# Uneven column parts in the tail of a two-stage attention and soft-MoE kernel: 288 + 224 instead of 256 + 256, and eight instead of twelve row blocks stored by parts

## The chip, the cores and the metric

The kernel runs on one core of a Trainium2 chip. Its engines work side by side and meet through semaphores: PE multiplies matrices, DVE and ACT do elementwise work and move results out of PSUM, POOL (GpSimd) masks and issues the loads that convert types, and SP issues the stores. Sixteen DMA engines move all the data between memory and the core's SBUF. The metric is the device time of one execution in microseconds (us).

## What is computed

Inputs are q, k and v of 4 batches x 8 heads x 768 positions x 64 columns. The first stage is an attention in which every query keeps 6 of 24 chunks of 32 keys, chosen by an upper bound on the score. Its output, as 3072 tokens x 512 columns, goes into a soft mixture of experts:

```
logits = x @ phi                      # 3072 x 32: 8 experts, 4 slots each
slot_input = softmax over tokens(logits).T @ x
for e in range(8):
    h = relu(slot_input[e] @ w1[e])   # w1[e]: 512 x 1024
    slot_out[e] = h @ w2[e]           # w2[e]: 1024 x 512
out = softmax over slots(logits) @ slot_out    # 3072 x 512, float32
```

So no output row can be formed before all slots are known, since each token mixes all 32 of them; and each column of `slot_out` needs the same column of all eight `w2`. The kernel uses the last point: the output can be finished for some columns while the weights of the other columns are still on their way. 6.29 MB of output are stored at the end.

## The kernel before

The work goes in 16 pairs of heads. For each pair, lists of step names (`PLAIN`, `REST`, ..., `FINAL`) set by hand in which order the instructions are put into the engines' queues. All this runs until about 121 us of the span; the change touches only what comes at the end.

Weights are loaded by POOL's queue, which also converts them from float32 to bfloat16. Fourteen of the sixteen matrices (`w1` of all experts, `w2` of the first six in the order `LATE`) come whole. The last two, `w2` of the experts 7 and 4, come in eight pieces, `load_w_half(0)` to `(7)` (L160): first the columns y = 1 (the right part) of both, then the columns y = 0 of both, each part in two pieces of 512 rows. Pieces 0 to 3 are issued from the lists of the last two pairs (`lh:0` to `lh:3`), pieces 4 to 7 after them. All pieces wait their turn in one queue.

The tail runs so, in the order of PE's queue:

- `experts_in` (L932): slot input times `w1`, in two halves of the hidden columns, with `relu` on ACT and `hidden_T` between.
- Part y = 1: `experts_out(1, f)` (L973) for the four experts with whole columns of the PE array, `shared_out(1, f)` (L999) for three experts that are spread over the column groups (the second-last of them from the pieces `w_half`), `last_expert_out(1)` (L1009) for the very last expert, all summed in `so_ps`. ACT scales the sum into the bfloat16 `so_sb[1]` (L1059).
- `out_half(m, 1, ...)` (L1046) for the first `BYHALF` entries of `ROWS`: PE mixes the slots for 128 tokens at a time, DVE and ACT in turn scale the result into the SBUF tile `o_rows` (L1029, L1026), SP stores it (L1050).
- Part y = 0 in the same way, from `experts_out(0, f)` on, summed in `so_last`, scaled on DVE (L1068); then `out_half(m, 0, ...)` for the same rows.
- The remaining rows in full width, 512 columns at once (PE L1078, store L1081). After the first of these, `last_rows` prepares the factors of the last batch: six transposes (L548), their copy on DVE (L556), six sums (L823) and a reciprocal (L959).

`ROWS` lists (first block of 128 tokens, number of blocks). In a group of w blocks, token p*w + x of the group sits in partition p, so a store of full rows writes w x 2048 bytes in one run per partition, and a store of one column part writes runs of its own width. The entry decides the size of the packets that the DMA engines handle.

```
    ROWS = [(2 * m, 2) for m in range(4)] + [(8, 4), (12, 2), (14, 4), (18, 6)]
    BYHALF = 5
```

With this, 12 blocks of 128 rows are stored by column parts (each of them twice, 256 columns or 1024 bytes wide) and 12 blocks in full. SP has 14 stores: 5 of part y = 1, 6 of part y = 0, 3 of full rows.

Of the kernel before, what the change touches and what calls it, by code (L numbers as in the profile page):

```python
# [9 lines left out]
F32 = mybir.dt.float32  # L10
BF16 = mybir.dt.bfloat16
# [9 lines left out]
P = 128  # L21
# [38 lines left out]
def kernel(  # L60
# [15 lines left out]
    Dm, NS = moe_phi.shape  # L76
    E, F = moe_w1.shape[0], moe_w1.shape[2]
    SPE = NS // E
    LATE = [0, 1, 2, 3, 5, 6, 7, 4]
    NDG, NFG = Dm // P, F // P  # L80
    EARLY = 14
    LAST = NPAIR - 1
    WIN, HOME = 6 * SPE, 4 * SPE

    ctx.enter_context(tc.manual_schedule())
    static = ctx.enter_context(tc.tile_pool(name="static", bufs=1))
# [2 lines left out]
    p_sc = ctx.enter_context(tc.tile_pool(name="p_sc", bufs=2, space=PSUM))  # L89
    p_at = ctx.enter_context(tc.tile_pool(name="p_at", bufs=1, space=PSUM))  # L90
# [15 lines left out]
    w_sb = []  # L106
# [45 lines left out]
    w_half = {}  # L152
# [3 lines left out]
    def load_w_half(n):  # L156

        e, y, a = HALVES[n]
        src = moe_w2[e].rearrange("(a p x) d -> a p x d", p=P, x=4)
        nc.gpsimd.dma_start(  # L160
            out=w_half[e, y][:, 4 * a:4 * a + 4, :], in_=src[a, :, :, y * Dm // 2:(y + 1) * Dm // 2])

    def load(i, nm, n=1):

# [18 lines left out]
    for t, src in zip(stage, (k, q)):  # L183
# [4 lines left out]
        out=ident, in_=ident, compare_op=ALU.not_equal, fill=1.0, base=0,  # L188
# [623 lines left out]
            return False  # L812
        return True

    ROWS = [(2 * m, 2) for m in range(4)] + [(8, 4), (12, 2), (14, 4), (18, 6)]

    def tokens(t0, w, x):
        return cT_all[:, t0:t0 + w].rearrange("p n c -> p (n c)").rearrange("p (k x) -> p x k", x=w)[:, x]

    def col_sums(ps, b):  # L820
        cols = [(t0, w, x) for t0, w in ROWS if t0 // NQT == b for x in range(w)]
        for n, c in enumerate(cols):
            nc.tensor.matmul(ps[:, n:n + 1], lhsT=tokens(*c), rhs=live, start=True, stop=True)  # L823
# [4 lines left out]
    for i in range(1, NPAIR):  # L828
        if i == NPB + 1:
            nc.vector.tensor_reduce(live, once, axis=AX.X, op=ALU.max)  # L830
        if i >= EARLY:
            wt = ctx.enter_context(tc.tile_pool(name=f"wt{i}", bufs=1))
            for y in range(2):
                w_half[LATE[i - E], y] = wt.tile([P, NFG, Dm // 2], BF16, name=f"w_half{i}_{y}")
        order = FINAL if i == LAST else BEFORE_LAST if i == LAST - 1 else PLAIN if i <= NPB else (
            REST, LOGITS, SLOTS, AFTER)[i % NPB]
        for what in order.split():
            if what.startswith("lh:"):
                load_w_half(int(what[3:]))
# [23 lines left out]
    for n in range(4, len(HALVES)):  # L863
        load_w_half(n)
# [19 lines left out]
    for n, part in enumerate((high(mneg), mneg_lo)):  # L884
        nc.tensor.matmul(
            lg2, lhsT=part.broadcast_to([NS, P]), rhs=rep.broadcast_to([NS, NQT, NS]),
            start=False, stop=(n == 1), skip_group_check=True,
# [34 lines left out]

    h_sb = tail.tile([P, 2, 512], BF16, name="h_sb")
    so_all = tail.tile([P, Dm], BF16, name="so_all")
    so_sb = [so_all[:, y * Dm // 2:(y + 1) * Dm // 2] for y in range(2)]
    h_ps.append(p_sc.tile([P, 2, 512], F32, name="h_ps1", tag="sc"))

    def experts_in(f, g):
# [26 lines left out]
    def last_rows():  # L955
        moe_ct(BL)
        ps = p_tp.tile([P, NQT], F32, name="cs_ps", tag="tp")
        col_sums(ps, BL)
        nc.vector.reciprocal(inv_b, ps)  # L959

    HD = Dm // 2
    so_ps = p_at.tile([P, 2, 512], F32, name="so_ps", tag="at")[:, 0, :HD]
    so_last = p_sc.tile([P, HD], F32, name="so_last", tag="sc")

    hT = hT_pad.rearrange("p f e c -> p f (e c)")

# [2 lines left out]
    def experts_out(y, f):  # L969
        for fg in range(f * 4, (f + 1) * 4):  # L970
            for e in range(4):
                w0 = fg * Dm + y * HD
                nc.tensor.matmul(  # L973
                    outs[y][e * CH:(e + 1) * CH, :], lhsT=hT_pad[:, fg, e, :],
                    rhs=w_sb[E + e][:, w0:w0 + HD], start=(fg == 0), stop=False,
                )

    SHARED = [
# [6 lines left out]
    def window(e, j):  # L985
        return e * CH + HOME - (e - j) * SPE

    def shared_out(y, f):
        for n in range(3):
            for j in range(4):  # L990
                e, fg = SHARED[j][n]
                fg += f * 4
                c0 = window(e, j)
                if e == LATE[-2]:
                    rhs = w_half[e, y][:, fg, :]
                else:
                    w0 = fg * Dm + y * HD
                    rhs = w_sb[E + LATE.index(e)][:, w0:w0 + HD]
                nc.tensor.matmul(  # L999
                    outs[y][j * CH:(j + 1) * CH, :], lhsT=hT[:, fg, c0:c0 + CH],  # L1000
                    rhs=rhs,
                    start=False, stop=False,
                )

    def last_expert_out(y):
        for fg in range(NFG):
            j = fg % 4
            c0 = window(LATE[-1], j)
            nc.tensor.matmul(  # L1009
                outs[y][j * CH:(j + 1) * CH, :], lhsT=hT[:, fg, c0:c0 + CH],  # L1010
                rhs=w_half[LATE[-1], y][:, fg, :],
                start=False, stop=(fg >= NFG - 4),
            )
# [9 lines left out]
    homes = {"sc": p_sc, "tp": p_tp, "at": p_at}  # L1023
# [6 lines left out]

    w_ctx.close()
    op = ctx.enter_context(tc.tile_pool(name="op", bufs=1))
    BYHALF = 5
    o_tiles = [op.tile([P, w, Dm], F32, name=f"o_rows{t0}") for t0, w in ROWS]

    def rows(m):
        t0, w = ROWS[m]
        return out[t0 * P:(t0 + w) * P, :].rearrange("(p x) d -> p x d", x=w)

    def out_half(m, y, tags):  # L1040
        cols = slice(y * HD, (y + 1) * HD)
        t0, w = ROWS[m]
        for x in range(w):
            tag = tags[m % 2 ^ x // 2][x % 2]
            ps = homes[tag].tile([P, HD], F32, name="oh_ps", tag=tag)
            nc.tensor.matmul(ps, lhsT=tokens(t0, w, x), rhs=so_sb[y], start=True, stop=True)  # L1046
            (scaled_dve, scaled_act)[x % 2](o_tiles[m][:, x, cols], ps, t0 + x)
            if x == w - 1 or x % 2 and y == 0:
                xs = slice(x - 1 if y == 0 else 0, x + 1)
                nc.sync.dma_start(out=rows(m)[:, xs, cols], in_=o_tiles[m][:, xs, cols])  # L1050

    experts_out(1, 0)
    shared_out(1, 0)
    hidden_T(1)
    slot_sums()
    experts_out(1, 1)
    shared_out(1, 1)
    last_expert_out(1)
    nc.scalar.activation(so_sb[1], outs[1], func=ACT.Copy, scale=zinv)  # L1059
    TAGS = (("tp", "tp"), ("sc", "at"))  # L1060
    for m in range(BYHALF):
        out_half(m, 1, TAGS)
    for f in range(2):
        experts_out(0, f)
    for f in range(2):
        shared_out(0, f)
    last_expert_out(0)
    nc.vector.tensor_scalar_mul(so_sb[0], outs[0], zinv)  # L1068
    for m in range(BYHALF):
        out_half(m, 0, TAGS)  # L1070

    n = 0
    for m in range(BYHALF, len(ROWS)):
        t0, w = ROWS[m]
        for x in range(w):
            tag = ("sc", "tp", "tp", "sc", "at")[n % 5]
# [4 lines left out]
        nc.sync.dma_start(out=rows(m), in_=o_tiles[m])  # L1081
        if m == BYHALF:
            last_rows()
# [30 lines left out]
```

## Time and profile before

| what | us |
|---|---|
| median of 3 runs (156.21 to 156.38) | 156.22 |
| the profiled execution | 155.95 |
| its span, first to last instruction | 154.2 |
| PE busy (89% of the span) | 136.8 |
| ACT busy (79%) | 121.5 |
| DVE busy (78%) | 120.4 |
| POOL busy (63%) | 97.5 |

Times in the views count from the start of the span. The profile names each DMA queue: q0 is POOL's (loads), q1 is SP's (stores, and two loads at the very start). A view of a stretch gives the number of packets, their bytes and rate, and each queue's share of the time of all 16 DMA engines; a share over 100% means that packets overlap on an engine. Sizes count the bytes written, so a converting load reads twice what is shown. "Time to landing" counts from the issue of a DMA until its last data is confirmed. The chain of waits is followed back from the last instruction: at each step to what released it.

### The profile page before, as it was taken

What the parts mean: (1) busy time and instruction counts of PE and PEld (TensorE: products, weight loads), DVE (VectorE), ACT (ScalarE), POOL (GpSimd) and SP (SyncE); (2) the same over time, 40 slices, a digit from 0 to 9 for tenths busy, and PEclk for the clock granted to TensorE, in tenths of its full rate; (3) what the DMA queues carried; (4) which work ended last, traced back from release to release, by engine and by line L of the source; (5) the groups of instructions that cost most, each with busy time, mean ns of one, the idle gap of its engine ahead of it and who ended that gap; (6) DMA issues with size and microseconds to landing.
All of it is one profiled execution on the core that took longest, in us unless ns stands there. A gap on an engine that the chain in (4) does not pass through costs nothing.

```text
span 154.2 us, 6098 instructions
## 1 busy us (share of the span) xinstructions
PE 136.8 (89%) x2513; PEld 91.6 (59%) x2513; DVE 120.4 (78%) x445; ACT 121.5 (79%) x167; POOL 97.5 (63%) x200
## 2 busy tenths in 40 slices
PE   7889999999999998999999799999989899776700
PEld 2444566767667686666667575767767655453300
DVE  4777988989899998999999999999767551449710
ACT  3678999999999999899999979999997133428700
POOL 6966698974976798885847938794694971000000
PEclk9999999999999999999999999999999999999975
DMA  4999999999999999999999999999999999999996
GB/s 140 207 188 206 206 189 194 215 179 196 209 217 193 199 205 189 198 205 212 205 190 198 209 202 199 206 184 213 217 191 218 211 197 198 181 266 353 371 429 255
DMA packets 45579, 33.31 MB, mean 216 GB/s; under 512 B 26224, under 2 KB 41584, under 8 KB 45296
## 3 DMA queue, kind: packets, MB, share of 16 engines
q0 software_dynamic: 41328, 25.86, 115.4%
q1 hardware_dynamic: 4224, 7.08, 12.5%
q8 instruction: 19, 0.31, 0.7%
q14 instruction: 8, 0.07, 0.1%
HBM read 52.49 MB, written 6.29 MB: 381 GB/s over the span
## 4 chain that ended last, share of the span: by engine, by line
PE 55%; POOL 13%; DMA 9%; DVE 8%; issue 5%; ACT 5%; DVEq 0%; SPq 0%; POOLq 0%; ACTq 0%
PE at_ps L382 12%; PE sc_ps L334 12%; PE sc_ps L344 9%; DMA w_half<-in_moe_w_dram 7%; PE tr_ps L225 6%; PE xT_ps L404 4%; POOL e_sb L368 4%; ACT e_sb L358 3%; PE ub_ps L284 3%; DMA w_sb<-in_q_dram 2%; PE ns_ps L316 2%; POOL v_t L174 2%; DVE o_rows L1029 2%; POOL w_half L160 1%; POOL w_sb L150 1%
## 5 line engine op out<-in xcount | busy, mean ns | idle before, releaser
L358 ACT ACTIVATE e_sb<-sc_ps 128x1024 bf16<-128x1024 f32 (+2 forms) x96 | 83.2, 932 | 4.7 <-PE sc_ps L344 4.5
L368 POOL TENSOR_SCALAR_AFFINE_SELECT e_sb<-e_sb 128x256 bf16<-128x256 bf16 x96 | 37.9, 415 | 15.6 <-ACT e_sb L358 15.2
L334 PE MATMUL sc_ps<-qT,kT 64*128 64x384 bf16 (+3 forms) x260 | 37.5, 306 | 0.7 <-ACT e_sb L358 0.6
L344 PE MATMUL sc_ps<-nsT,smask 64*128 64x384 bf16 (+2 forms) x296 | 37.6, 284 | 0.1
L382 PE MATMUL at_ps<-v_t,e_sb 128*128 128x65 bf16 x630 | 25.9, 193 | 1.0 <-DVE x_sb L395 0.8
L382 PEld LDWEIGHTS <-e_sb 128*128 128x128 bf16 x630 | 22.0, 97 | 5.1 <-issue 4.0
L305 DVE MAX8 mx<-ub_ps 128x8 f32<-128x8 f32 (+1 forms) x192 | 16.9, 165 | 5.6 <-PE ub_ps L294 5.1
L334 PEld LDWEIGHTS <-kT 64*128 64x128 bf16 x260 | 13.5, 93 | 8.4 <-issue 1.8
L174 POOL DMA_DIRECT2D v_t<-in_v_dram x16 | 16.9, 1056 | 1.1 <-PE sc_ps L344 0.9
L344 PEld LDWEIGHTS <-smask 64*128 64x128 bf16 x296 | 14.9, 95 | 3.1 <-issue 0.4
L395 DVE TENSOR_TENSOR x_sb<-at_ps,inv 128x768 bf16<-128x768 f32 (+3 forms) x18 | 15.6, 869 | 0.6
L244 DVE TENSOR_REDUCE mm<-kT 128x24 bf16<-128x768 bf16 x16 | 15.1, 944 | 0.1
L250 DVE TENSOR_REDUCE mm<-kT 128x24 bf16<-128x768 bf16 x16 | 15.1, 943 | 0.0
L235 ACT COPY qT<-tr_ps 128x768 bf16<-128x768 bf16 x16 | 13.0, 813 | 1.5 <-PE tr_ps L225 1.5
L235 ACT COPY kT<-tr_ps 128x768 bf16<-128x768 bf16 (+1 forms) x16 | 12.7, 793 | 0.6 <-PE tr_ps L225 0.6
L150 POOL DMA_DIRECT2D w_sb<-in_moe_w_dram x14 | 10.1, 724 | 0.0
L415 DVE COPY xT_sb<-xT_ps 128x768 bf16<-128x768 bf16 (+1 forms) x16 | 8.6, 535 | 2.0 <-PE xT_ps L404 2.0
L215 PE MATMUL warm_ps<-ones_sq 128*128 128x512 bf16 x27 | 8.7, 446 | 1.1 <-DVE ones_sq L180 1.1
L284 PEld LDWEIGHTS <-qpn 128*128 128x128 bf16 x192 | 6.1, 96 | 4.9 <-issue 3.8
L284 PE MATMUL ub_ps<-bd,qpn 128*128 128x48 bf16 x192 | 7.9, 184 | 0.8 <-issue 0.5
L404 PE MATMUL xT_ps<-ident,x_sb 128*128 128x128 bf16 x96 | 8.4, 220 | 0.0
L1026 ACT ACTIVATE o_rows<-oh_ps,inv_a 128x256 f32<-128x256 f32 x12 | 5.0, 470 | 3.5 <-PE oh_ps L1046 2.7
(171 smaller groups left out, 222.9 us busy)
## 6 DMA issues: line engine op xcount, KB each, us to landing
w_sb<-in_moe_w_dram POOLq DMA_DIRECT2D x14, 1024.0 KB, 18.3
v_t<-in_v_dram POOLq DMA_DIRECT2D x16, 192.0 KB, 15.1
out_dram<-o_rows SPq DMA_DIRECT2D x10, 256.0 KB, 3.0
w_half<-in_moe_w_dram POOLq DMA_DIRECT2D x8, 256.0 KB, 11.2
k_in<-in_k_dram POOLq DMA_DIRECT2D x5, 384.0 KB, 13.3
q_in<-in_q_dram POOLq DMA_DIRECT2D x5, 384.0 KB, 12.3
out_dram<-o_rows SPq DMA_DIRECT2D x1, 1536.0 KB, 6.0
out_dram<-o_rows SPq DMA_DIRECT2D x2, 512.0 KB, 3.9
```

The costliest lines, as they stand in the source:

```text
L174: nc.gpsimd.dma_start(out=v_t[i % NV][:, :, :, :D], in_=v[b, 2 * j:2 * j + 2].rearrange("h (g p) d -> p h g d", p=P),)
L235: copy(t.rearrange("d (p g) -> d p g", g=NQT)[:, :, g0:g1], ps.rearrange("d g p -> d p g"),)
L244: nc.vector.tensor_reduce(mm[:, 0, 0, :], kT, axis=AX.X, op=ALU.min)
L250: nc.vector.tensor_reduce(mm[:, 1, 0, :], kT, axis=AX.X, op=ALU.max)
L284: nc.tensor.matmul(o, lhsT=qpn[:, x, t * P:(t + 1) * P], rhs=bd[:, x], start=(t == 0 and x == 0), stop=False,)
L305: nc.vector.max(mx[:, a, :], ub[:, a, :max(8, 4 * t + 4)])
L334: nc.tensor.matmul(ps[:, h, c:c + w], lhsT=kT[r, kg * P:(kg + 1) * P], rhs=qT[r, qs], start=True, stop=False,)
L344: nc.tensor.matmul(ps[:, h, c + (f - t0) * P:c + (l - t0) * P], lhsT=smask[r, x, kg].rearrange("p a b -> p (a b)"), rhs=nsT[r, (f - x * NJ ...
L358: nc.scalar.activation(e[:, :, :w], st.pop(("scps", i, g))[:, :, :w], func=ACT.Exp, scale=scale)
L368: nc.gpsimd.affine_select(out=e[:, :, c:c + P], in_=e[:, :, c:c + P], compare_op=ALU.is_ge, fill=0.0, base=0, pattern=[[0, 2], [1, P]], ch ...
L382: nc.tensor.matmul(o, lhsT=st["e", i, g][:, h, c:c + P], rhs=v_t[i % NV][:, h, kg, :D + 1], start=(kg == 0), stop=(kg == t),)
L395: nc.vector.tensor_tensor(st["x", b][:, t0:t1, 2 * j:2 * j + 2, :].rearrange("p t h d -> p h t d"), at[:, :, :, :D], inv.broadcast_to([P, ...
```

## The change

The last two weights are cut at column 224 instead of 256: y = 0 gets columns 0 to 223, y = 1 columns 224 to 511. The first-loaded part y = 1 is thus 288 columns wide, the last-loaded part 224. All tiles, matmuls and stores of a part take its width. `ROWS` is cut anew: six groups of 2 blocks, then 4, 2 and 6; the first four groups (8 blocks) are stored by parts, the other 16 blocks in full. For y = 1, the first group's two blocks are stored one by one; for the others one store per group. And the 32 matmuls `experts_out(0, f)` are moved on PE's queue from behind the first part's output to a place ahead of `last_expert_out(1)`.

```
+    COLS = [slice(0, 224), slice(224, Dm)]
+    CW = [c.stop - c.start for c in COLS]
...
-            out=w_half[e, y][:, 4 * a:4 * a + 4, :], in_=src[a, :, :, y * Dm // 2:(y + 1) * Dm // 2])
+            out=w_half[e, y][:, 4 * a:4 * a + 4, :], in_=src[a, :, :, COLS[y]])
...
-    ROWS = [(2 * m, 2) for m in range(4)] + [(8, 4), (12, 2), (14, 4), (18, 6)]
+    ROWS = [(2 * m, 2) for m in range(6)] + [(12, 4), (16, 2), (18, 6)]
...
-                w_half[LATE[i - E], y] = wt.tile([P, NFG, Dm // 2], BF16, name=f"w_half{i}_{y}")
+                w_half[LATE[i - E], y] = wt.tile([P, NFG, CW[y]], BF16, name=f"w_half{i}_{y}")
...
-    so_sb = [so_all[:, y * Dm // 2:(y + 1) * Dm // 2] for y in range(2)]
+    so_sb = [so_all[:, c] for c in COLS]
...
-    HD = Dm // 2
-    so_ps = p_at.tile([P, 2, 512], F32, name="so_ps", tag="at")[:, 0, :HD]
-    so_last = p_sc.tile([P, HD], F32, name="so_last", tag="sc")
+    so_ps = p_at.tile([P, 2, 512], F32, name="so_ps", tag="at")[:, 0, :CW[1]]
+    so_last = p_sc.tile([P, CW[0]], F32, name="so_last", tag="sc")
...
-                w0 = fg * Dm + y * HD
+                w0 = fg * Dm + COLS[y].start
                 nc.tensor.matmul(
                     outs[y][e * CH:(e + 1) * CH, :], lhsT=hT_pad[:, fg, e, :],
-                    rhs=w_sb[E + e][:, w0:w0 + HD], start=(fg == 0), stop=False,
+                    rhs=w_sb[E + e][:, w0:w0 + CW[y]], start=(fg == 0), stop=False,
...
-    BYHALF = 5
+    BYHALF = 4
...
-        cols = slice(y * HD, (y + 1) * HD)
+        cols = COLS[y]
...
-            ps = homes[tag].tile([P, HD], F32, name="oh_ps", tag=tag)
+            ps = homes[tag].tile([P, CW[y]], F32, name="oh_ps", tag=tag)
...
-            if x == w - 1 or x % 2 and y == 0:
-                xs = slice(x - 1 if y == 0 else 0, x + 1)
+            if x == w - 1 or m == 0 and y == 1:
+                xs = slice(x if m == 0 and y == 1 else 0, x + 1)
                 nc.sync.dma_start(out=rows(m)[:, xs, cols], in_=o_tiles[m][:, xs, cols])
...
     experts_out(1, 1)
     shared_out(1, 1)
+    for f in range(2):
+        experts_out(0, f)
     last_expert_out(1)
     nc.scalar.activation(so_sb[1], outs[1], func=ACT.Copy, scale=zinv)
     TAGS = (("tp", "tp"), ("sc", "at"))
     for m in range(BYHALF):
         out_half(m, 1, TAGS)
-    for f in range(2):
-        experts_out(0, f)
     for f in range(2):
         shared_out(0, f)
     last_expert_out(0)
```

More of the change, by code (lines that the diff above doesn't have):

```diff
@@ L996, in shared_out @@
                 else:
-                    w0 = fg * Dm + y * HD
-                    rhs = w_sb[E + LATE.index(e)][:, w0:w0 + HD]
+                    w0 = fg * Dm + COLS[y].start
+                    rhs = w_sb[E + LATE.index(e)][:, w0:w0 + CW[y]]
                 nc.tensor.matmul(
```

## The prediction

> **What bounds the kernel now.** I read the page's slices first, for the engine that is full while the kernel ends; then the chain of waits over the tail, then the stores on SP's queue, then the DMA queues stretch by stretch.
>
> ```profile
> DMA  4999999999999999999999999999999999999996
> GB/s 140 207 188 206 206 189 194 215 179 196 209 217 193 199 205 189 198 205 212 205 190 198 209 202 199 206 184 213 217 191 218 211 197 198 181 266 353 371 429 255
> ```
>
> Busy tenths and rate of the DMA engines in 40 slices: they are full in every slice but the first and the last, and the rate doubles in the last ones, where stores replace loads. The chain of waits, from the last weight on:
>
> ```profile
> 127.14 10.44 DMA w_half<-in_moe_w_dram
> 137.63 0.32 PE so_last L1009 x4
> 137.97 0.49 DVE so_all L1068
> 138.51 0.41 PE oh_ps L1046 x2
> 138.94 0.84 ACT o_rows L1026 x2
> ...
> 144.54 2.06 DVE o_rows L1029 x3
> ```
>
> The last weight piece lands at 127.14 + 10.44 = 137.58; 1.86 us later (139.44) SP issues the first store of the second column part. SP's queue at the first store of the first part, the first of the second, and the last store of all:
>
> ```profile
> 134.09 0.62 SPq L1050 DMA_DIRECT2D out_dram<-o_rows  x1
> 139.44 0.53 SPq L1050 DMA_DIRECT2D out_dram<-o_rows  x1
> 147.33 0.33 SPq L1081 DMA_DIRECT2D out_dram<-o_rows  x1
> out_dram<-o_rows SPq DMA_DIRECT2D x1, 1536.0 KB, 6.0
> ```
>
> The last store lands at 147.33 + 6.0 = 153.33, 6.7 us after the last DVE work (144.54 + 2.06): what ends the kernel is store data, not arithmetic. The DMA view for 134 to 137, for 137.5 to 144.5, and from 152.5 on:
>
> ```profile
> DMA packets 794, 0.52 MB, mean 173 GB/s; under 512 B 31, under 2 KB 793, under 8 KB 793
> q0 software_dynamic: 566, 0.28, 70.6%
> q1 hardware_dynamic: 227, 0.22, 21.3%
> ...
> DMA packets 2544, 2.47 MB, mean 352 GB/s; under 512 B 135, under 2 KB 2544, under 8 KB 2544
> q1 hardware_dynamic: 2544, 2.47, 102.4%
> ...
> DMA packets 17, 0.01 MB, mean 7 GB/s; under 512 B 16, under 2 KB 16, under 8 KB 16
> ```
>
> So there is a handover with unused capacity (173 GB/s), then store packets of 1024 B without a hole at 352 GB/s through 140, where the stores change from the first part to the second, and the data ends about 152.9. Part one's backlog lasts exactly until part two's rows come. In bytes: 0.22 MB stored by 137, then 0.35 MB per us, is 1.49 MB at 140.6, against the 1.57 MB (1536 rows of 1024 B) that part one has. That is the place to watch.
>
> **The change part by part.** Prices of store packets first. SP's last issue of column parts and the first two of full rows, each with its time to landing (the last is above):
>
> ```profile
> 142.77 0.51 SPq L1050 DMA_DIRECT2D out_dram<-o_rows  x1
> out_dram<-o_rows SPq DMA_DIRECT2D x1, 256.0 KB, 3.0
> 143.38 0.66 SPq L1081 DMA_DIRECT2D out_dram<-o_rows  x1
> out_dram<-o_rows SPq DMA_DIRECT2D x1, 512.0 KB, 3.8
> 145.35 0.34 SPq L1081 DMA_DIRECT2D out_dram<-o_rows  x1
> out_dram<-o_rows SPq DMA_DIRECT2D x1, 1024.0 KB, 4.3
> ```
>
> They land at 145.8, 147.15, 149.65 and 153.33: 1.33 us for 128 packets of 4096 B, 2.5 for 8192 B, 3.7 for 12288 B. With 16 engines, a 1024 B packet takes an engine 16 x 1024 / 352 = 46.5 ns, one of 12288 B 3700 / 8 = 462 ns. A line through both: 8.7 ns a packet and 0.0369 ns a byte. So 1152 B (288 columns) takes 51.2 ns and 896 B (224 columns) 41.8 ns, together 93.0 = 2 x 46.5: the uneven split itself is free in the stores.
>
> *Rows by parts.* Before: 12 x 128 rows twice, 192 packets per engine, 8.93 us; then 1.33 + 2.5 + 3.7; 16.46 in all. After: 64 x 93.0 ns = 5.95 us, three groups of 4096 B packets (4.0), 2.5 and 3.7; 16.15. Gain 0.31 us of DMA work (four groups of 128 rows cost 16 long packets instead of 64 short ones).
>
> *Weights.* The first part's pieces get rows of 288 columns, the second's 224; the bytes stay. What packet size does to the loading queue is seen in three stretches: long rows mostly (116 to 122), 512 B packets (126 to 133.5), and many of the 128 B rows of v among long ones (113 to 115.8):
>
> ```profile
> DMA packets 336, 1.31 MB, mean 218 GB/s; under 512 B 20, under 2 KB 20, under 8 KB 335
> ...
> DMA packets 2910, 1.47 MB, mean 196 GB/s; under 512 B 86, under 2 KB 2907, under 8 KB 2908
> ...
> DMA packets 1273, 0.56 MB, mean 199 GB/s; under 512 B 1176, under 2 KB 1176, under 8 KB 1272
> ```
>
> An engine takes 41.8 ns for 512 B and about 301 ns for 4096 B: 4.8 ns a packet and 0.072 a byte. Thus 576 B costs 46.4 ns and 448 B 37.2: the four first pieces (128 packets per engine) end 0.6 us later, the four last take that back. The last weight lands at 137.58 as before.
> The Trainium skill (DMA: Bandwidth & Descriptors, Specifications) says that transfers under 512 B are read, modified and written, which speaks against the 448 B rows. By it they would cost up to twice as much, 128 x 37 ns = 4.7 us more, an estimate. The trace disagrees: 1176 packets under 512 B among 1273 leave the rate at 199 GB/s. So I give it no chance of its own.
>
> *A row of 288 columns starts at byte 896.* All rows moved so far start at multiples of 512 B at least on the memory side (or are whole 256 B rows of v), so no row prices this start. Bounds: nothing, or one more packet's fixed cost each, as if the packet were cut in two: 128 x 4.8 ns = 0.6 us on the weights and 64 x 8.7 = 0.56 on part one's stores, which are off the path (below). A gain is excluded: no packet becomes shorter by it. I take 0, since the fitted cost is nearly all bytes, and keep 0.6 for the range.
> The Trainium skill (same page, How a descriptor splits into AXI transactions) says that a descriptor that starts off a 256 B boundary also fetches the bytes below its start: here 128 B more for 1152, so 40 beats instead of 36. By it the weights would end 128 x 46.4 x 4/36 = 0.66 us later, an estimate; no row of this trace has such a start.
>
> *PE, first part.* These rows carry it: the fourth weight piece's issue and landing, its matmuls, the 32 matmuls that move ahead of them, and the evacuations:
>
> ```profile
> 120.26 0.74 POOL L160 DMA_DIRECT2D w_half<-in_moe_w_dram  x1
> w_half<-in_moe_w_dram POOLq DMA_DIRECT2D x1, 256.0 KB, 12.0
> 131.93 0.63 PE L1009 MATMUL so_ps<-w_half,hT_pad 128*32 128x256 bf16 x8
> 135.52 1.06 PE L973 MATMUL so_last<-w_sb,hT_pad 128*32 128x256 bf16 x32
> 132.60 0.47 ACT L1059 ACTIVATE so_all<-so_ps,zinv 128x256 bf16<-128x256 f32 x1 [2.21 <-PE so_ps L1009]
> ```
>
> The piece landed at 132.2 and its matmuls ended at 132.56, so they already waited on it. After, it lands at 132.8. The 32 moved matmuls take about 0.8 us of PE at 224 columns, from 132.0 (0.1 later for wider shared matmuls) to 132.8: they fill that wait. If the weights came as early as before, the move would cost the first stores those 0.8 us. Behind them on PE stand the last eight matmuls of part one, on ACT the scaling L1059 that waits for these, and behind that all of part one's stores. All of it comes 0.6 us later; the first store goes out near 134.7 instead of 134.1 (two issues of 128 rows, so the first waits for DVE alone).
> What hides this delay is the loading queue: in 134 to 137 it still moves 0.28 MB, 94 GB/s of the 196 it had, so about half of its engines carry weights, the latest until about 137.2 (an estimate, ahead of the landing at 137.58). For these, store data is waiting either way. For the engines that are free earlier it is idle time.
>
> *From first part to second.* How long from SP's issue to data? The first packets of q1 after the issue at 134.09 are seen in the stretch 135.35 to 135.4 (none in 135.2 to 135.35); those after SP's first load of the kernel in 1.9 to 1.95:
>
> ```profile
> q1 hardware_dynamic: 5, 0.01, 28.6%
> ...
> 0.81 0.44 SPq L184 DMA_DIRECT2D w_sb<-in_k_dram  x1
> q1 hardware_dynamic: 6, 0.01, 289.0%
> ```
>
> So 1.26 us and 1.1; I take 1.26, which is a store of the same size, and keep 1.1 for the lower end. The second part's chain shortens by its narrower columns, priced from
>
> ```profile
> L1026 ACT ACTIVATE o_rows<-oh_ps,inv_a 128x256 f32<-128x256 f32 x12 | 5.0, 470 | 3.5 <-PE oh_ps L1046 2.7 <-DMA w_half<-in_moe_w_dram 0.5
> L1026 ACT ACTIVATE o_rows<-o_ps,inv_a 128x512 f32<-128x512 f32 x3 | 2.0, 685 | 1.5 <-PE o_ps L1078 1.5
> L1029 DVE TENSOR_SCALAR o_rows<-o_ps,inv_a 128x512 f32<-128x512 f32 x3 | 2.2, 748 | 0.4 <-PE o_ps L1078 0.4
> ```
>
> 0.84 ns a column, 32 columns: 0.03 on ACT, as much on DVE's so_all, 0.02 on PE; 0.09 in all. The first store of part two is issued at 139.35, its data starts at 139.35 + 1.26 = 140.6. Part one has 64 x 51.2 ns = 3.28 us per engine now: engines free of weights early finish about 135.9 + 3.3 = 139.2, the latest, from 137.2 on, at 140.5. All are dry when part two starts; before, part one's backlog reached 140.8. This is what the change loses.
>
> *Sum.* From 140.6: 64 x 41.8 ns = 2.67, three groups of 4096 B packets 4.0, then 2.5 and 3.7: 12.87, ending at 153.5. The same account for before: 3.15 - 1.49 = 1.65 MB at 352 GB/s = 4.70, and 1.33 + 2.5 + 3.7: 12.23 from 140.6, ending at 152.83 (seen: 152.9). That is +0.6. With the lower latency 1.1 and store packets of 4096 B at 3.8 for three, it is +0.25. I take +0.5.
>
> *What hides the rest.* Evacuation: 16 parts and 16 full rows instead of 24 halves and 12 full; two rows of 512 columns take 0.75 us of DVE beside ACT, their data 1.33: covered. The last batch's transposes and sums now stand one group earlier, ahead of rows 1280:
>
> ```profile
> 142.42 0.47 DVE cT_all L556
> ...
> 142.94 0.44 PE cs_ps L823 x6
> ```
>
> About 1 us lies between the groups for it; the DMA queue then holds part two's 2.67 us and a 4096 B group. If that cover were gone, the next group would start up to 1 us late. SP: 14 issues as before. Part two's went out 0.67 apart (five intervals from 139.44 to 142.77), so four take 2.67, as long as their data: just enough. POOL issues the same eight weight pieces.
>
> The profiled execution took 155.95, its span is 154.2; the median of the runs is 156.22, 0.27 above. The difference is put on the median: 156.7.
>
> **The rivals.**
> *Faster: the backlog holds.* If part one's stores still last until part two's data (latest engines at 140.5, data at 140.4 with the short latency), only these engines decide, and the 0.31 of DMA work is gained: 155.9. For it: the weights leave the engines over some 3 us (94 GB/s in 134 to 137) while store data ends on all of them by 152.9, so the late ones may set the pace. Against: in 137.5 to 144.5 all 16 engines are busy (102.4%), so none has time in reserve. It decides from the point where the hole is under 0.3 us on the mean engine.
> *Same: a hole half as long,* 0.3 us, gives back what the longer packets save: 156.1 to 156.5.
> *Slower by more: the off-boundary start costs.* The last weight lands up to 0.6 later, and the whole second part with it, on top of +0.5: 157.0 to 157.4. For it only that no row has such a start; against, the queue's price is almost all bytes.
>
> **How the numbers follow.** Forecast (dry engines, aligned price) 0.45, own range 156.5 to 156.9; off-boundary 0.17; same 0.20; faster 0.18. Range: from the faster case's 155.8 to 157.3. About 0.2% (0.31 us) is what a measurement can tell: faster 0.18, same 0.21, slower 0.61.
>
> **What would show it.** Right: the stretch 139.2 to 140.6 shows q1 well under 352 GB/s; the last piece lands near 137.6; first part-two issue near 139.35; store data ends near 153.4. Wrong: no dip there (the faster rival), the last piece at 138 or later (the off-boundary start), or a later hole before the 4096 B groups (evacuation or SP's issues too slow).

## The result, and the profile after

The changed kernel takes 157.5 us (median; 157.01 to 158.57), the kernel before, run beside it, 156.38 (155.73 to 157.71). The ratio is 1.0066, with a 95% interval of 1.0042 to 1.0090: about 1.0 us slower. (Ratios, here and below, leave out executions more than 1.5% above the fastest of the same kernel, and are not the quotient of the medians.) The direction is the forecast's, the size is twice the +0.5 it took, and 157.5 lies above the range's 157.3. The profiled execution took 157.09 with a span of 155.4; that of before, on which the forecast was built, took 155.95 with 154.2. Both lie some 0.4 below the median of their kernel, so the two traces, 1.14 apart, can be set side by side, with one reserve: in the second the last weight landed 0.66 us later (below).

The slices of the page, after (40 equal parts of the span, busy tenths and rate of the DMA engines):

```profile
DMA  4999999999999999999999999999999999979996
GB/s 153 193 185 206 205 191 196 215 177 195 212 216 191 196 208 189 197 204 215 202 191 202 203 208 197 202 187 219 206 199 219 207 201 194 156 205 340 418 422 253
```

One slice that was full is no longer full (a 7, the fifth from the end). The rate is 156 GB/s ahead of it and 205 in it, where before has 181 and 266. The slices behind it, 340, 418, 422 and 253, are together no slower than before's 353, 371, 429 and 255. The DMA view of the changed kernel for 134 to 137 and for 137.5 to 144.5, the stretches that the prediction shows of before:

```profile
DMA packets 761, 0.41 MB, mean 136 GB/s; under 512 B 664, under 2 KB 760, under 8 KB 760
q1 hardware_dynamic: 107, 0.11, 11.2%
...
DMA packets 2144, 2.26 MB, mean 323 GB/s; under 512 B 139, under 2 KB 2072, under 8 KB 2144
q1 hardware_dynamic: 2136, 2.26, 95.7%
```

The stores (q1) got 0.11 MB through in the first stretch instead of 0.22, and in the second 2.26 MB in all went instead of 2.47. The windows show where (length, busy times and counts of PE, its weight loads, DVE, ACT, POOL, then granted PE clock, DMA share, GB/s); after:

```profile
124.00:126.00 2.00, 2.00 (x35) 1.17 (x37) 1.41 (x7) 0.83 (x2) 1.58 (x3) 0.51 1.24 201
126.00:128.00 2.00, 2.00 (x28) 0.80 (x24) 0.10 (x2) 0.00 (x0) 0.74 (x1) 0.64 1.42 204
...
134.00:136.00 2.00, 1.15 (x8) 0.68 (x8) 1.07 (x3) 1.40 (x4) 0.00 (x0) 1.00 0.93 124
136.00:138.00 2.00, 1.11 (x30) 0.71 (x30) 0.76 (x2) 0.87 (x2) 0.00 (x0) 1.00 0.67 162
138.00:140.00 2.00, 0.90 (x9) 0.57 (x9) 1.02 (x3) 0.47 (x2) 0.00 (x0) 1.00 0.82 262
...
140.00:141.00 1.00, 1.00 (x6) 0.51 (x6) 1.00 (x3) 0.98 (x4) 0.00 (x0) 1.00 1.03 323
```

and before:

```profile
134.00:136.00 2.00, 1.80 (x28) 1.18 (x31) 1.90 (x5) 1.90 (x6) 0.00 (x0) 1.00 1.01 171
136.00:138.00 2.00, 1.63 (x56) 1.22 (x44) 0.17 (x2) 0.21 (x1) 0.00 (x0) 1.00 0.93 266
138.00:140.00 2.00, 1.25 (x8) 0.81 (x9) 1.62 (x4) 1.05 (x3) 0.00 (x0) 1.00 1.02 355
```

So the hole is there, but it stands at 136 to 138.5, ahead of the place the prediction named (139.2 to 140.6), where the engines are full. In this execution part one itself began late: the PE clock was granted at 0.51 and 0.64 in 124 to 128, and PE came to the 32 moved matmuls only at 132.82, when the fourth weight piece was about to land (132.85). Instead of filling a wait they now held up the last eight matmuls of part one, to 133.59, and the first store went out at 135.58 instead of the forecast 134.7. SP's queue, after: first store of part one, first of part two, last of all, each with its time to landing:

```profile
135.58 0.36 SPq L1051 DMA_DIRECT2D out_dram<-o_rows  x1
...
140.00 0.53 SPq L1051 DMA_DIRECT2D out_dram<-o_rows  x1
out_dram<-o_rows SPq DMA_DIRECT2D x1, 224.0 KB, 2.4
148.21 0.33 SPq L1082 DMA_DIRECT2D out_dram<-o_rows  x1
out_dram<-o_rows SPq DMA_DIRECT2D x1, 1536.0 KB, 6.2
```

The last store lands at 154.41, 1.08 later than before's 153.33. Between the first store of part two and the last store 8.21 us pass, before 7.89. The chain of waits, after, from the last weight on:

```profile
127.14 11.10 DMA w_half<-in_moe_w_dram
...
138.28 0.30 PE so_last L1010 x4
...
138.61 0.46 DVE so_all L1069
...
139.12 0.28 PE oh_ps L1047
```

From landing (138.24) to issue (140.00) it is 1.76 us; the forecast had 1.77. But the landing is 0.66 later than the 137.58 of before. How much was stored by the time part two's data starts, about 141.1, says the rest. Queue q1 in 133 to 141 (packets, MB, share), before:

```profile
q1 hardware_dynamic: 1676, 1.64, 59.3%
```

and after:

```profile
q1 hardware_dynamic: 1025, 1.11, 43.2%
```

Part one now has only 1.18 MB (1024 rows of 1152 B). Wherever the hole stands, no more than these can be stored before part two's data comes, while before had stored 1.64 MB by 141. The 0.53 MB that are missing take 1.35 us at the 391 GB/s that before held from 141 on ((6.29 - 1.64) MB from 141 to 152.9); the longer packets of the full rows give back 0.3 of them. That is 1.05, against the 1.14 seen. This account of two single traces has the later landing in it; how far the ends of both kernels move with the landing is seen below, from more traces.

### The profile page after: what moved, and what is told of

The parts are those of the page before. It is cut to its first block, busy times and chain, and to the rows that moved or that the text cites. A ratio compares the mean times of both kernels' runs of the same rounds, so it can differ in the third digit from the quotient of the medians.

```text
span 155.4 us, 6085 instructions
## 1 busy us (share of the span) xinstructions
PE 137.3 (88%) x2509; PEld 90.8 (58%) x2509; DVE 120.0 (77%) x443; ACT 121.0 (78%) x165; POOL 97.3 (63%) x200
## 3 DMA queue, kind: packets, MB, share of 16 engines
HBM read 52.49 MB, written 6.29 MB: 378 GB/s over the span
## 4 chain that ended last, share of the span: by engine, by line
PE 60%; DVE 10%; DMA 10%; POOL 8%; issue 4%; ACT 3%; DVEq 0%; SPq 0%; POOLq 0%; ACTq 0%
PE sc_ps L336 13%; PE at_ps L384 13%; PE sc_ps L346 10%; DMA w_half<-in_moe_w_dram 7%; PE tr_ps L227 7%; PE xT_ps L406 4%; PE ub_ps L286 3%; DVE o_rows L1030 3%; ACT e_sb L360 3%; PE ns_ps L318 3%; DMA w_sb<-in_q_dram 2%; POOL w_half L162 1%; POOL e_sb L370 1%; POOL v_t L176 1%; PE lg_ps L429 1%
## 5 line engine op out<-in xcount | busy, mean ns | idle before, releaser
L310 DVE TENSOR_TENSOR ns_t<-ub_ps,mx 128x288 bf16<-128x288 f32 x16 | 7.3, 458 | 0.5
```

## Experiments

The theory to be tested is that of the forecast, a dry store queue between part one and part two. Its rivals put the loss on the uneven split (rows that start off a 256 B boundary), on the moved matmuls, on the last weights that land later because stores compete with them, and on the sums that now stand one group earlier.

### The three parts of the change, one at a time

*Only the new groups of rows, columns still 256 + 256* (before, with):

```
-    ROWS = [(2 * m, 2) for m in range(4)] + [(8, 4), (12, 2), (14, 4), (18, 6)]
+    ROWS = [(2 * m, 2) for m in range(6)] + [(12, 4), (16, 2), (18, 6)]
-    BYHALF = 5
+    BYHALF = 4
-            if x == w - 1 or x % 2 and y == 0:
-                xs = slice(x - 1 if y == 0 else 0, x + 1)
+            if x == w - 1 or m == 0 and y == 1:
+                xs = slice(x if m == 0 and y == 1 else 0, x + 1)
```

> Before with the new ROWS alone (8 blocks by parts, columns 256 + 256, matmuls where they were). Theory A, the stores run dry between the parts: part one has 64 packets of 46.5 ns per engine (2.98 us), done by about 140.2 on the latest engines and 138.4 on the early ones, part two's data from 140.6; 0.5 to 0.9 us slower than before, with the queue of stores well under 352 GB/s in 138.5 to 140.6. Theory B, the cost comes from rows that start at byte 896 (none here): 0.3 us faster, from the longer packets. Theory C, the cost comes from the matmuls moved on PE's queue: 0.3 us faster as well.

Measured: ratio 1.0063 [1.0029, 1.0096], the whole loss. The DMA view of this kernel for 139.5 to 141.5 (40 slices of 0.05 us):

```profile
DMA  9999998641100000000000000000268999999999
GB/s 328 328 430 348 328 348 307 226 164 62 61 21 0 0 0 0 0 0 0 0 0 0 0 0 0 0 0 0 102 225 307 348 328 328 369 348 348 348 328 369
```

From 139.9 to 140.9 the engines are all but empty: the hole that the prediction placed at 139.2 to 140.6. There is no uneven split and no moved matmul in this kernel. It stored 1.07 MB in 133 to 141, like the changed kernel: the stores run dry because eight blocks are too few. The sums stand earlier in this kernel too. Its trace shows no hole behind them, but its other executions were not traced, so the ratio holds whatever the sums cost as well.

*Only the move of the 32 matmuls:*

```
+    for f in range(2):
+        experts_out(0, f)
     last_expert_out(1)
...
-    for f in range(2):
-        experts_out(0, f)
```

> Before with the 32 matmuls of part two moved ahead of last_expert_out(1) alone. A: part one's stores start 0.6 to 0.9 us later, their 12 blocks still last until part two's data; within 0.3 us of before. B: the same as before. C: part one's first store goes out 0.9 us later and the time rises by 0.5 to 1.0.

Measured: 1.0002 [0.9968, 1.0035], and 1.52 MB stored in 133 to 141. The move costs no time, as forecast. This trace shows something else, though: in an execution whose PE clock was granted at 0.5 from about 140.7 to 147.5, the kernel with twelve blocks and the sums at their old place has a partly empty stretch behind the sums:

```profile
147.00:148.00 1.00, 0.99 (x4) 0.18 (x2) 0.90 (x2) 0.87 (x2) 0.00 (x0) 0.76 0.63 262
```

*Only the split 288 + 224, twelve blocks by parts as before* (the lines of the diff that have `COLS` and `CW`):

> Before with columns 288 + 224 alone (12 blocks by parts in the old ROWS, matmuls where they were). A: part one's backlog is longer than before, nothing runs dry; within 0.2 us of before. B: 96 packets of 1152 B per engine at the 57 ns seen in the changed kernel instead of 51.2: 0.55 us slower. C: the same as before.

Measured: 1.0010 [0.9977, 1.0043]. The weights carry no price of the odd start. The DMA view for 126 to 132.8, where the last weights load (q0); first this kernel (576 B and 448 B packets), then before (512 B):

```profile
q0 software_dynamic: 2525, 1.31, 141.6%
```

```profile
q0 software_dynamic: 2633, 1.31, 144.0%
```

Both move the same 1.31 MB in the stretch: for these loads what a packet costs goes by its bytes, wherever it starts. The last weight landed at 138.13.

*Split and rows, without the move* (the changed kernel with `experts_out(0, f)` back at its old place):

> The changed kernel with the 32 matmuls put back behind part one's output. A: like the changed kernel, 0.5 to 1.0 us slower than before, since the queue runs dry all the same. B: 64 x 5.8 ns slower and 0.3 faster, together the same as before. C: the loss is gone, 0 to 0.3 us faster than before.

Measured: 1.0060 [1.0026, 1.0093], no different from the rows alone. The window 140 to 141 of this kernel is empty (3% busy, 12 GB/s):

```profile
140.00:141.00 1.00, 1.00 (x8) 0.47 (x7) 0.94 (x3) 0.99 (x4) 0.00 (x0) 1.00 0.03 12
```

### How many blocks go by column parts

The changed kernel with `BYHALF` 6, 5 and 3 in place of 4, that is 12, 10 and 6 blocks of 128 rows by column parts instead of 8:

```
-    BYHALF = 4
+    BYHALF = 6
```

> The changed kernel with 12 blocks by column parts instead of 8 (same groups of two blocks, columns 288 + 224, matmuls moved). A: part one has 96 packets of 57 ns per engine again, 5.5 us, which lasts until part two's data; the queue of stores shows no hole and the loss is gone but for 0.1 to 0.3 us of shorter packets: 0 to 0.3 us slower than before. If instead the loss came from the split, the groups of two blocks or the moved matmuls, it stays at 0.7 to 1.0 us.

> The changed kernel with 10 blocks by parts. A: 16 packets of 57 ns per engine more than in the changed kernel, 0.9 us of its hole of about 1.1 us filled, less 0.15 for shorter packets: 0.2 to 0.5 us slower than before. Without A: as the changed kernel, 1.0 slower.

> The changed kernel with 6 blocks by parts. A: the hole grows by 16 packets, 0.9 us, less 0.15 for longer packets: 0.7 us slower than the changed kernel, 1.7 slower than before. If longer packets are what counts, 0.15 us faster than the changed kernel.

Measured: 12 blocks 1.0042 [1.0008, 1.0076], 10 blocks 1.0136 [1.0093, 1.0178], 6 blocks 1.0144 [1.0095, 1.0194]. With 12 there is no hole between the parts, with 6 a longer one. The windows of 12 blocks:

```profile
140.00:141.00 1.00, 0.78 (x4) 0.39 (x4) 1.00 (x4) 0.99 (x4) 0.00 (x0) 1.00 1.05 338
```

and of 6 blocks:

```profile
140.00:141.00 1.00, 1.00 (x6) 0.63 (x5) 0.76 (x2) 0.57 (x2) 0.00 (x0) 0.50 0.10 35
141.00:142.00 1.00, 0.89 (x4) 0.29 (x3) 0.52 (x2) 0.93 (x3) 0.00 (x0) 0.50 0.00 0
```

That much follows the dry queue. The sizes fit less well. The 12 blocks were expected at 0 to 0.3 us over before and lost 0.42%, about 0.7 us. The 6 blocks were expected at 1.7 and lost about 2.2; their trace has a second hole behind the sums (DMA share 0.39 and 0.74 in 145 to 147), so their loss is not the longer first hole alone. The 10 blocks should lie between 8 and 12, and are slower than both (6 and 10 blocks were timed four times each). The windows of 10 blocks:

```profile
138.00:140.00 2.00, 1.44 (x16) 0.74 (x9) 0.88 (x3) 0.24 (x1) 0.00 (x0) 0.50 1.04 337
140.00:141.00 1.00, 0.98 (x5) 0.47 (x4) 0.94 (x4) 0.93 (x3) 0.00 (x0) 0.50 1.04 336
...
146.00:147.00 1.00, 1.00 (x4) 0.38 (x3) 1.00 (x2) 1.00 (x3) 0.00 (x0) 1.00 0.02 4
```

The hole between the parts is closed (1.04 at 140 to 141), and a second one has opened at 146, behind the sums. The timeline there, 10 blocks (start, duration; in brackets the idle time before and what ended it):

```profile
142.59 0.82 PE L550 MATMUL cT_ps<-ident,c_pad 128*128 128x128 bf16 x6
...
143.50 0.55 DVE L558 COPY cT_all<-cT_ps 128x768 bf16<-128x768 bf16 x1
...
143.65 0.48 SPq L1082 DMA_DIRECT2D out_dram<-o_rows  x1
...
144.10 0.44 PE L825 MATMUL cs_ps<-live,cT_all 128*128 128x1 bf16 x6 [0.69 <-DVE cT_all L558]
...
144.83 1.85 ACT L1027 ACTIVATE o_rows<-o_ps,inv_a 128x512 f32<-128x512 f32 x3 [2.00 <-PE o_ps L1079]
...
146.52 0.34 SPq L1082 DMA_DIRECT2D out_dram<-o_rows  x1
```

PE stands in its order: the transposes (L550) and sums (L825) of the last batch come ahead of the next rows, so ACT waits 2.00 us for them. The next store is one of four blocks, all of which must be evacuated first: it is issued 2.87 us after the one before, and the engines had by then nothing left. This kernel had its PE clock granted at 0.5 from 136.4 to 143.2.

### Where the split lies

The kernel before, its columns split at 192 instead of 256, so that the first part's rows are 1280 B and start at byte 768, a multiple of 256:

```
+    COLS = [slice(0, 192), slice(192, Dm)]
```

> The split of the columns alone, at 192 instead of 224: rows of 1280 B that start at byte 768, a multiple of 256. If the off-boundary start is what makes the 1152 B store packets take 55 to 58 ns instead of 51.2, these take 56 by the line of the page before (8.7 + 1280 x 0.0369 = 55.9), no longer than the shorter ones. If it is the width, they take 62 or more. Part one is long enough: within 0.3 us of before.

Measured: 1.0046 [1.0022, 1.0070]. It is slower as a whole, by more than the 0.3 us expected, and why was not followed further: it was run for the price of its packets. The DMA view for 138.5 to 140, first the split at 224 alone (1152 B from byte 896), then the split at 192:

```profile
q1 hardware_dynamic: 461, 0.51, 103.1%
```

```profile
q1 hardware_dynamic: 450, 0.54, 99.5%
```

Share times 1.5 us times 16 engines over packets is 53.7 ns for 1152 B and 53.1 ns for 1280 B; before it is 45.0 ns for 1024 B in the same stretch (544 packets, 101.9%). (All three means take in a few packets of under 512 B, 21 to 29 of them.) With 0.0369 ns a byte, 1152 B should take 49.7 and 1280 B 54.4. The rows that start at byte 896 cost about 4 ns more than their size (52.9 to 55.7 ns in the same stretch of 12 blocks and of the changed kernel, so 3 to 6 ns), the aligned ones nothing. On 96 packets per engine, as in the kernel with 12 blocks, 4 ns would be 0.4 us, part of its 0.42%. But the split alone stores the same 96 packets and lost 0.10% [-0.23, 0.43]: the times neither show this price nor exclude it.

### Do the stores delay the last weights?

The changed kernel and the one before, each without the stores of part one:

```
-                nc.sync.dma_start(out=rows(m)[:, xs, cols], in_=o_tiles[m][:, xs, cols])
+                if y == 0:
+                    nc.sync.dma_start(out=rows(m)[:, xs, cols], in_=o_tiles[m][:, xs, cols])
```

> The changed kernel without the stores of part one (the output columns 224 to 511 of the first 1024 rows are left out; its time is not read). Question: why did the last weight piece land at 138.24 instead of 137.58? Theory L, part one's stores share engines with the last weights and slow them: it lands at 137.6 or before here, 1.15 to 1.2 us after the piece ahead of it. Rival N, it is the rows of 224 columns or chance: 138 or later, as in the changed kernel.

> The kernel before without the stores of part one (output columns 256 to 511 of the first 1536 rows are left out; its time is not read). L: the last weight piece lands at 137.4 to 137.6, 1.34 us after the piece ahead of it, as before or a little sooner. N: no difference to e9.

The last weight in the chain of waits, changed kernel without these stores:

```profile
127.94 10.47 DMA w_half<-in_moe_w_dram
```

and before without them:

```profile
127.92 10.48 DMA w_half<-in_moe_w_dram
```

They land at 138.41 and 138.40, later than with the stores, and alike in both kernels. So neither the stores nor the change is needed for a late landing. The issue varies most: 127.14 in the two first traces, 127.9 here. From issue to landing it is 10.44 before, 11.10 after, and 10.47 and 10.48 here. The time behind the piece ahead, Theory L's other sign, is 1.36 before and 1.87 after, and 1.24 and 1.39 without the stores. So for the first trace after, whose last piece alone came late, it is not excluded that stores held it up; two executions cannot tell. In all traces of this study the landing lies between 137.58 and 138.86, changed or not. The two kernels as they are, profiled once more with these:

> The kernel before once more, for another trace. If the profile that the prediction used was an average one, the last weight lands at 137.5 to 137.7 and the first store of part one goes out near 134.1. If it was a lucky one, the landing is 0.2 us or more later and the first store too.

> The changed kernel once more. If the late start of part one's stores (135.58 in its first trace) and the low clock at 124 to 127.4 were chance, the first store goes out near 134.7 and the hole stands at 139.5 to 141 instead of 136 to 138.5, with about the same total and the same end. If they belong to the change, they are here again.

Before took 156.25 and has a partly empty stretch of its own. Its DMA view for 139.5 to 141.5:

```profile
DMA  9999999999999999999754324222246999999999
GB/s 410 410 348 328 348 369 369 369 348 369 369 369 348 369 348 328 369 348 430 246 185 164 123 102 164 82 82 102 82 143 246 328 348 369 348 369 348 348 348 328
```

Its last weight landed at 137.95, 0.37 later than in the forecast's trace:

```profile
127.46 10.49 DMA w_half<-in_moe_w_dram
```

In this execution even twelve blocks do not quite last: "without a hole", as the prediction read it, does not hold for every execution. The changed kernel took 158.11, and its windows show both holes:

```profile
140.00:141.00 1.00, 1.00 (x6) 0.60 (x4) 0.86 (x3) 0.85 (x3) 0.00 (x0) 0.50 0.25 82
...
142.00:145.00 3.00, 2.33 (x12) 1.02 (x12) 1.68 (x5) 1.15 (x2) 0.00 (x0) 0.50 0.99 366
145.00:146.00 1.00, 1.00 (x3) 0.30 (x2) 0.90 (x2) 0.83 (x2) 0.00 (x0) 0.50 0.26 107
```

The first stands where it was forecast, the second behind the sums, in a stretch in which the PE clock was granted at 0.5 (139.8 to 146.6). Its last weight and its last store:

```profile
127.57 10.47 DMA w_half<-in_moe_w_dram
149.46 0.33 SPq L1082 DMA_DIRECT2D out_dram<-o_rows  x1
out_dram<-o_rows SPq DMA_DIRECT2D x1, 1536.0 KB, 6.0
```

Counted from the landing of the last weight to that of the last store, the traces fall into three groups:

| execution | last weight lands | last store lands | between |
|---|---|---|---|
| before | 137.58 | 153.3 | 15.7 |
| before, profiled again | 137.95 | 153.6 | 15.7 |
| before, without part one's stores | 138.40 | 154.1 | 15.7 |
| changed | 138.24 | 154.4 | 16.2 |
| changed, timed again (below) | 138.11 | 154.5 | 16.4 |
| changed, without part one's stores | 138.41 | 154.8 | 16.4 |
| changed, profiled again: second hole | 138.04 | 155.5 | 17.4 |

Both kernels end later when the weight lands later, before by as much as after. From the same landing the changed kernel is 0.5 to 0.7 us behind, and 1.0 to 1.2 more in the execution with the second hole.

### The sums one group later

The kernel with 10 blocks (first pair of lines) and the changed kernel (second pair), with the sums put behind a later group of rows; the changed kernel twice, the second time beside another timing of itself:

```
-        if m == BYHALF:
+        if m == BYHALF + 1:
...
-        if m == BYHALF:
+        if m == BYHALF + 2:
```

> The kernel of e6 (10 blocks by parts) with the last batch's transposes and sums one group later, behind the group of four blocks. If e6 lost its second us to the hole at 146 to 147, where the next group waited for rows that stand behind the sums on PE, DVE and ACT, that hole closes and the time falls by about 1.1 us, to 0.2 to 0.6 slower than before. If e6 was slow for the number of blocks, it stays at 2 us slower than before.

> The changed kernel with the same move of the sums (behind the group of four blocks). Its first trace shows no hole after 141.5, its second one of 1.3 us. If the hole between the parts alone is the loss, within 0.3 us of the changed kernel, 0.7 to 1.0 slower than before. If the second hole matters on the mean, 0.3 to 0.6 us faster than the changed kernel.

> The changed kernel, timed on the same chip as e18: 0.9 to 1.2 us slower than before, as in the result.

> The kernel of e14 on the same chip as e17. If the sums ahead of the next group cost about half of the loss, 0.4 to 0.6 us faster than e17 and 0.4 to 0.6 slower than before. If e14 was a favourable draw, no faster than e17 by more than 0.2.

Measured: 10 blocks 1.0044 [1.0001, 1.0088] instead of 1.0136. Changed kernel with later sums 1.0029 [1.0005, 1.0054] and 1.0017 [0.9988, 1.0046]; the changed kernel itself again 1.0052 [1.0019, 1.0084]. The window of the second hole, 10 blocks with later sums:

```profile
146.00:147.00 1.00, 1.00 (x5) 0.55 (x5) 0.66 (x1) 1.00 (x2) 0.00 (x0) 1.00 0.99 410
```

It was 4 GB/s and is 410, with the clock at 0.5 from 140.3 on in this execution too. So the place of the sums makes the second hole; for 10 blocks the intervals do not overlap, and the cost in time is shown. For the changed kernel the intervals overlap, but the long executions are gone: over 157.5 us are 13 of its 29 timed ones, and none of the 22 with later sums. In the same comparison the mean falls by 0.45 us (157.44 to 156.99), the median by 0.2 (157.31 to 157.11). Later sums leave the first hole as it was (140 to 141 moves 77 GB/s in the last of these traces): 0.17% to 0.29% are still lost, where the first value's interval includes no loss.

### Can the kernel before gain?

*More blocks by parts in the kernel before* (14 instead of 12), for a backlog that surely lasts:

```
-    BYHALF = 5
+    BYHALF = 6
```

> The kernel before with 14 instead of 12 blocks by parts, same groups. If a backlog of stores that lasts until part two's data is what counts, and the kernel before has a hole of 0.35 us in an average execution (its second trace), the 16 more packets of 46.5 ns fill that: 0.35 gained, 0.3 lost to shorter packets: the same as before within 0.2 us. If more blocks by parts are better throughout, 0.5 us faster; if shorter packets are all that counts, 0.3 us slower.

Measured: 1.0064 [1.0015, 1.0113], 156.69 to 160.95. Its profile still has a short idle time between the parts (0.26 us of the mean engine in 139 to 141.5). The edit also moves the sums to stand directly ahead of the last group, so what makes it slower was not told apart: inconclusive.

*Smaller groups of full rows in the kernel before, sums a group later:*

```
-    ROWS = [(2 * m, 2) for m in range(4)] + [(8, 4), (12, 2), (14, 4), (18, 6)]
+    ROWS = [(2 * m, 2) for m in range(4)] + [(8, 4), (12, 2), (14, 2), (16, 2), (18, 6)]
-        if m == BYHALF:
+        if m == BYHALF + 1:
```

> The kernel before with its full group of four blocks cut into two of two, and the last batch's sums behind the first of these instead of ahead of it. If the hole behind the sums also costs the kernel before something in its slower executions, its mean falls by 0.2 to 0.5 us; if it has no such hole, 0.1 us slower for the shorter packets (8 x 312 ns against 16 x 162).

Measured: 1.0011 [0.9980, 1.0043]. With twelve blocks by parts later sums gain nothing on the mean, although the trace of the moved matmuls shows that a hole behind the sums can occur there too. No version that was run beats the kernel before.

## Why the prediction was right or wrong

**Right: the mechanism, the sign and the price of the first hole.** Stores run dry between part one and part two because part one holds eight blocks instead of twelve. The rows alone give the whole loss (1.0063), 12 blocks close the hole, 6 widen it. From the same landing the changed kernel ends 0.5 to 0.7 us later, where "Sum" had +0.6 and took +0.5; with the sums moved later the measured loss is 0.3 to 0.45 us.

**Right: the terms around it.** The fourth piece of the weights was to land 0.6 later, through its width: it did (132.85 against 132.22), and 1152 B rows load as fast as 1024 B rows (1.31 MB either way in 126 to 132.8). Rows of 448 B load at the old rate. The move costs no time (1.0002). The chain from the last weight to part two's first store takes 1.76 (forecast 1.77). From part two's first data, about 141.1, to the end at 154.1 it is 13.0 (forecast 12.87).

**The step that failed: "What hides the rest", the sums one group earlier at nothing.** The prediction named the cover (part two's 2.67 us and one group of 4096 B packets) and the price if it were gone, up to 1 us, and then added nothing for it. The cover was enough where PE had its full granted clock in this stretch (the changed kernel's first trace, and that of its second timing, have no second hole) and not where the clock was granted at 0.5: the second trace has the hole at 145 and ends 17.4 us after the landing instead of 16.2 to 16.4, and 10 blocks lost more than a microsecond to it (1.0136 against 1.0044 with later sums). For the changed kernel, putting the sums later removes 0.2 us of the median, 0.45 of the mean and 0.35% (0.55 us) of the ratio, measured side by side, and all executions over 157.5. That is about half of the 1.0 us. The intervals overlap, so this division is an estimate.

**Early for both kernels: the start at 140.6 in "Sum".** That time was the landing at 137.58, plus the chain, plus 1.26. The landing of 137.58 was the earliest of this study; the others lie at 137.7 to 138.9, with the change and without it. The two first traces are 1.14 apart because the second landed 0.66 later; 0.48 is left. The account by bytes has this in it: the prediction compared 1.49 MB (before) with 1.18 (after) at 140.6, 0.31 MB or 0.9 us, less 0.3 for longer packets; at 141 of the first traces it is 1.64 against 1.11. Since the end of the kernel before moves with its landing as well (table above), a late landing does not by itself explain the average loss. Whether the change makes the landing later on average is not shown by so few traces. And having got +0.6, the prediction took +0.5 toward a low end that it had for a shorter latency.

**Off-boundary rows: right for loads, wrong for stores, and without weight here.** The bounds were 0 and one more packet's fixed cost; 0 was taken. The loads paid nothing. The stores of 1152 B paid about 4 ns each (3 to 6), half of the upper bound of 8.7. With 64 of them per engine that is 0.26 us ahead of a hole, which only becomes shorter by it; with 12 blocks, where there is no hole, it would be paid, but the times do not show it. The rule of the Trainium skill (DMA: Bandwidth & Descriptors, How a descriptor splits into AXI transactions) would make these packets 4/36 longer, an estimate of 5.5 ns on 49.7 for the stores; the traces agree with it nearly there (4 ns) and not for the loads.

**Wrong: the place of the dip in the first trace.** The prediction had it at 139.2 to 140.6, the trace after has it at 136 to 138.5, since part one started 0.9 later than forecast: PE, at half clock in 124 to 127.4, was late, and the moved matmuls then stood in the way for some 0.75 us, the price that the prediction gave for a PE that does not wait. The rows alone, without the move, had their first store at 134.57 with the clock at 0.56 and 0.59 in 124 to 128. The half clock is not the only way to it: the changed kernel's second timing had 1.00 there and its first store at 136.06. Other executions (the rows alone, split and rows, the changed kernel again) have it where it was forecast. The end does not depend on it, because part two's data sets it.

**The rivals.** "The backlog holds" and "a hole half as long" fell with the first traces; the sign for "the off-boundary start" (last piece at 138 or later) did appear, but it was no sign of that: in the first trace after, the off-boundary pieces landed on time (the fourth at 132.85, forecast 132.8), and without part one's stores the kernel before landed as late (138.40).

**Open.** Why the issue of the last weights varies (126.9 to 128.4 in all traces), and why the last piece then takes 10.4 to 11.1 us. Why SP's second or third issue of part one sometimes takes 1.1 us and more instead of 0.36. Whether the lower mean clock of the changed kernel's timed executions (0.965 against 0.975 to 0.978) belongs to the change or follows from its longer idle times. Why 14 blocks by parts were slower.

## What to carry to other kernels

Where a kernel ends in stores, count in bytes what can be stored before the next part's data exists: what is missing from that at the moment the data starts is paid, less what longer packets give back, wherever the hole shows. Take the moment from several executions: a queue that is just full in one trace is not full in the next. Compare two traces from the event that sets their ends, here the landing of the last weight, or its chance enters the difference. A step that is moved one group earlier in an engine's order needs its cover priced at the half clock too, if PE is on its path.

## What the hardware showed that was not expected

- A store packet of 1152 B from byte 896 took an engine 53.7 ns where its size asks for 49.7; 1280 B from byte 768 took 53.1 (54.4 by size). The 1152 B rows of weights from the same byte loaded at no extra cost.
- The granted PE clock falls to 0.5 for stretches of about 3.4 or 6.8 us (124.0 to 127.4, 136.4 to 143.2, 139.8 to 146.6), in some executions and not in others of the same kernel. The Trainium skill (TensorE: Matmul & The Clock Gate, Part 1: The HAM clock gate) has a window of 3413 ns and half rate after an idle one; the lengths agree. PE was busy through most of the stretches themselves, and no run here shows what starts them.
- A kernel with fewer blocks by column parts is not between its neighbours in time (10 blocks 1.0136, 8 blocks 1.0066, 12 blocks 1.0042): each number of blocks also places the sums at another spot in the order of the rows.
